# Windowed attention inside a feed-forward stream: nine score blocks in one group over two PSUM banks, values likewise, and the scheduler's constants set anew

## The chip, the core and the metric

The kernel runs on one core of one Trainium2 chip. The metric is the device time of one execution in microseconds (us). PE is TensorE's matmul stream, PEld its weight loads, DVE is VectorE, ACT ScalarE, POOL GpSimd, SP the engine whose queue issues most transfers. PSUM has eight banks of 512 fp32 columns.

## What is computed

Attention over 4 batches of 8 heads (576 positions, 64 columns a head), then two feed-forward layers (512 to 2048 to 512) over the 2304 tokens.

```python
scores = scale * q @ k.T
mask   = 0 <= rel < 32                          # heads 0..3
mask   = 0 <= rel < 128 and rel % 4 == 0        # heads 4..7
attn   = softmax(where(mask, scores, -1e9))
x      = (attn @ v) as tokens x 512
h = x @ w_in1;  x = (h - tanh(h)) @ w_out1
h = x @ w_in2;  y = (h * sigmoid(h)) @ w_out2
```

## The kernel before

**Layers.** Tokens go in blocks of 512 (the last of a layer has 256): blocks 0 to 4 are layer 1, five more are layer 2. For each of 16 slices `f` of the hidden width, a block does 12 matmuls of 512 columns into a bank `h` (four `c` of three passes each, since every operand is held as a high and a low part), a gate on ACT and DVE, and 12 matmuls from `gg` into the four banks `y`. All of these are issued in `passes` (L583).

**Attention.** Two heads make a `Pair`; four pairs make a batch. The 576 positions of a pair are cut into `NB` = 9 blocks of 64 queries by 96 keys. `products` (L444) makes score blocks on PE, one 64x64 matmul per head and block; `masks` (L465) scales and adds the mask on DVE, `maxima` (L468) takes the row maxima, `exps` (L481) the exponentials on ACT, `norm` (L486, L487, L491) divides, `p_transpose` (L504) turns the probabilities on DVE, `values` (L522) multiplies by v on PE, and `x_hi` (copy helper, L135) and `x_lo` (L563) write the result into `X`. Batch 0 goes in units of `UB` = 3 blocks and adds its masks on PE (L437). The later batches work in groups of three score blocks in the single bank of the pool `ps_s`, and values in groups of six and three blocks in the single bank of `ps_o`.

**Order.** Four things set it. Batch 0, block 0, all of batch 1 and the preparation of layer 1's weights (L169, L174, L179, L183, L135, L192: four engines take each chunk apart into high and low parts) are operations `op(...)` with an assumed cost per engine and a rank; `play` emits them in the order of a greedy schedule. While a bank is lent for it, `play` fills assumed idle time of PE with dummy matmuls (`idle`, L97). Batches 2 and 3 are laid into the stream of blocks 1 to 3 by `plan`: `STARTS` gives each pair's first tick (a tick is half a slice, 12 layer matmuls), `STEPS` the ticks of its steps after that. Before everything, `WARM` dummy matmuls (L799) run on PE. Weight chunks wait in staging buffers, one fixed and the others named by `MORE_OUT` and `MORE_IN`.

```python
at(s0 + score + u, lambda u=u: p.scores(u))
at(s0 + exp + u, lambda u=u: p.exps(u))
...
at(s0 + out, lambda: p.outputs(0, 2 * UB))
at(s0 + out + 1, lambda: p.outputs(2 * UB, NB))
```

Of the kernel before, what the change touches and what calls it, by code (L numbers as in the profile page):

```python
# [19 lines left out]
P = 128  # L20
# [3 lines left out]
UB = 3  # L24
# [8 lines left out]
def tile_kernel(  # L33
# [223 lines left out]
    tpool = attn.enter_context(tc.tile_pool(name="tiny", bufs=4))  # L257
# [7 lines left out]
    one = {}  # L265
    for dt in (F32, BF16):
        t = cpool.tile([P, P], dt, name=f"one{len(one)}")
        nc.gpsimd.memset(t, 0.0)
        keep(t, [[-1, P]], 0, 1, fill=1.0, op=ALU.not_equal)
        one[dt] = t  # L270


    mask = cpool.tile([P, NB + 2, KB], BF16, name="mask")
# [3 lines left out]
    keep(half, [[0, NB + 2], [-1, KB]], HALO, 1)  # L277
    keep(half, [[0, NB + 2], [1, KB]], -1, -1)
    for n in range(NB):

        for start in range(0, S, CLS):
            at = start - (QB * n - HALO)
# [5 lines left out]
    mask_dil = [mask[:, UB * u:UB * (u + 1)] for u in range(NU)]  # L288
    mask_plain = [mask[:, 0::5]] + [mask[:, NB - 1:]] * (NU - 1)

    late = cpool.tile([P, NC, SHIFT], F32, name="late")
# [5 lines left out]
    class Pair:  # L297
# [132 lines left out]
        def part(self, t, u):  # L430
            return t[:, UB * u:UB * (u + 1)]

        def products(self, bank, u, masked):
            s = bank[:, :UB * KB].rearrange("p (n k) -> p n k", n=UB)
            mk = (mask_dil if self.dil else mask_plain)[u]
            if masked:
                nc.tensor.matmul(s, one[BF16], mk, start=True, stop=False)  # L437
            for m in range(UB):
                n = UB * u + m
                k0 = QB * n - HALO  # L440

                for at, k1, size in ((0, k0, KB),) if n else ((0, 0, HALO), (HALO, 0, KB - HALO))[masked:]:
                    for j in range(2):
# [4 lines left out]
                            start=not masked, stop=not masked or m == UB - 1,  # L448
                        )
            if u == 0:  # L450
                self.p = ppool.tile([P, NB, KB], F32, tag="p", name="prob")
                self.total = tpool.tile([P, NB], F32, tag="sum", name="sum", bufs=2)
            self.nb[u] = tpool.tile([P, UB], F32, tag="nb", name="nb")
# [3 lines left out]
        def masked_scores(self, u, bank):  # L457
            self.ps[u], _ = self.products(bank, u, True)

        def plain_scores(self, u):  # L460
            self.ps[u] = self.products(ps_s.tile([P, 512], F32, tag="s", name="s"), u, False)

        def masks(self, u):
            s, mk = self.ps.pop(u)
            nc.vector.scalar_tensor_tensor(out=self.part(self.p, u), in0=s, scalar=SCALE, in1=mk, op0=ALU.mult, op1=ALU.add)  # L465

        def maxima(self, u):
            nc.vector.tensor_reduce(out=self.nb[u], in_=self.ps[u] if u in self.ps else self.part(self.p, u), axis=AX.X, op=ALU.max, negate=True)  # L468


        def scores(self, u):
            self.plain_scores(u)
            self.masks(u)
            self.maxima(u)

        def exps(self, u):
            s, nb = self.ps.pop(u, None), self.nb.pop(u)
            for m in range(UB):
                n = UB * u + m
# [262 lines left out]
    def plan(p, s0):  # L742
# [23 lines left out]
    with tc.manual_schedule():  # L766
# [60 lines left out]
        for i, (p, u) in enumerate(units):  # L827
# [27 lines left out]
            a = op({"T": 0.5}, lambda e, p=p, u=u, i=i: p.values(UB * u, UB * (u + 1), *((ps_s, "s") if i % 2 else (ps_o, "o"))),  # L855
# [46 lines left out]
        left_s = left_o = tuple(x_done[NPAIR - 1][-2:])  # L902
        left_pT = tuple(ring_v.take() + ring_v.take() + ring_v.take())
        left_qT = left_kT = left_v = ()
        left_v = (first[2].last,)
        x_next = []
        todo_v = None
        for p in pairs[NPAIR:2 * NPAIR + 1]:
            r = NEXT0 + NEXT * p.c + (NEXT * NPAIR if p.b > 1 else 0)
            q_in = op({"S": 2.2}, lambda e, p=p: p.load_q(), left_qT, r - 12, 2.0)  # L910
            k_in = op({"S": 2.2}, lambda e, p=p: p.load_k(), left_kT, r - 12, 2.0)
            hold = op({"P": 0.2}, lambda e, p=p: p.v_tile(), left_v, r - 5)
            v_in = [op({"S": 0.55}, fn, [hold], r - 5 + 0.01 * n, 0.4) for n, fn in enumerate(p.v_loads())]
            if p.b > 1:
                break
            a = op({"V": 1.09}, lambda e, p=p: p.transpose(0), [q_in, *left_qT], r)
            b = op({"V": 1.09}, lambda e, p=p: p.transpose(1), [k_in, *left_kT], r)
            free_p = ring_p.take()
            exps, scores = [], []
            for u in range(NU):  # L920
                c = op({"T": 0.65}, lambda e, p=p, u=u: p.plain_scores(u), [a, b, *left_s, *free_p], r + 2 + 2 * u)
                scores.append(c)
                d = op({"V": 0.46}, lambda e, p=p, u=u: p.masks(u), [c], r + 2 + 2 * u)
                left_s = (d,)
                d = op({"V": 0.4}, lambda e, p=p, u=u: p.maxima(u), [d], r + 2 + 2 * u)
                exps.append(op({"A": 1.35}, lambda e, p=p, u=u: p.exps(u), [d], r + 3 + 2 * u))
            left_qT = left_kT = tuple(scores)
            left_qT, left_kT = (a, *scores), (b, *scores)
            c = op({"V": 0.4}, lambda e, p=p: p.sums(0, NB), exps, r + 9)
            c = op({"V": 1.0, "P": 1.64}, lambda e, p=p: p.normed(e, 0, NB), [c], r + 9, port=True)  # L930
            ts = [op({"V": 0.4}, lambda e, p=p, j=j, n=n: p.p_quarter(j, n), [c, *left_pT], r + 11 + 0.5 * n)
                  for j in range(2) for n in range(4)]
            ring_p.leave(*ts)
            vals = []
            for n0, n1 in ((0, 2 * UB), (2 * UB, NB)):
                m = (n1 - n0) / NB
                a = op({"T": 1.5 * m}, lambda e, p=p, n0=n0, n1=n1: p.values(n0, n1), [*ts, *v_in, *left_o], r + 14)
                vals.append(a)
                b = op({"A": 0.2 + m}, lambda e, p=p, n0=n0: p.x_hi(e, n0), [a], r + 15)
                c = op({"V": 0.2 + m}, lambda e, p=p, n0=n0: p.x_lo(n0), [b], r + 15)  # L940
                left_o = (c,)
                x_next.append(c)
            left_pT = tuple(vals)
            left_v = tuple(vals)
# [22 lines left out]
        for f in range(NF):  # L967
# [17 lines left out]
            for f2 in ([f - 1] if f else []) + ([f] if f == NF - 1 else []):  # L985
                pass
        for f in range(NF - 2):
            prev = second[f - 1][-1:] if f else [x for p in (first[-1],) for x in x_done[NPAIR - 1]]
            for c in range(NC):
# [107 lines left out]
```

## Time and profile before

| what | us |
|---|---|
| median of 3 runs (lowest, highest) | 903.54 (903.01, 904.36) |
| the profiled execution's own time | 905.87 |
| its span, first to last instruction | 904.1 |
| PE busy | 887.0 (98%) |
| DVE, ACT, POOL busy | 423.2, 386.5, 130.2 |

The profiled execution lies 2.3 us above the median, and its span is 1.8 us shorter than its own time. The stretches of the span: 0 to 48.6 is batch 0; 48.6 to 162 is block 0 with batch 1 and the weight preparation; 162 to 362 holds blocks 1 to 3 with batches 2 and 3; from there the layers run alone.

### The profile page before, as it was taken

The numbers are of one execution on the slowest core, as the hardware profiler recorded it, in microseconds if no ns is written. First come the engines' busy times: TensorE is split into PE (matmuls) and PEld (weight loads), VectorE is DVE, ScalarE is ACT, GpSimd is POOL, SyncE is SP. The second block draws the span as 40 slices with busy tenths as digits, with TensorE's granted clock in tenths as the row PEclk, the third lists the DMA queues.
The fourth block names the chain that finished last, engine by engine and source line by source line (L and its number), as shares of the span: only waits on it lengthen the run. The fifth ranks groups of instructions, "written<-read, shape, count | busy, mean of one in ns | idle before, by whom it ended". The sixth has DMA issues, their size and how long they took to land.

```text
span 904.1 us, 13656 instructions
## 1 busy us (share of the span) xinstructions
PE 887.0 (98%) x5260; PEld 726.9 (80%) x5260; DVE 423.2 (47%) x782; ACT 386.5 (43%) x927; POOL 130.2 (14%) x168
## 2 busy tenths in 40 slices
PE   8899999999999999999998999999999999999998
PEld 5677777777777778888898888888888888888897
DVE  3569986556666654323365656522222222222232
ACT  5699974433343333332355666432223222322322
POOL 7455652000000000000011222100000000000000
PEclk9799999999999999999999999999999999999999
DMA  9967243421234200400164564140004000300100
GB/s 230 281 180 186 66 122 92 120 47 31 49 67 130 38 9 20 162 1 24 47 219 133 168 213 153 47 140 1 0 1 140 1 0 1 94 1 1 30 18 24
DMA packets 121313, 74.29 MB, mean 82 GB/s; under 512 B 84864, under 2 KB 106400, under 8 KB 121248
## 3 DMA queue, kind: packets, MB, share of 16 engines
q1 hardware_dynamic: 120416, 72.57, 28.7%
q0 software_dynamic: 832, 0.85, 0.4%
q8 instruction: 41, 0.67, 0.3%
q14 instruction: 24, 0.20, 0.1%
HBM read 59.24 MB, written 14.16 MB: 81 GB/s over the span
## 4 chain that ended last, share of the span: by engine, by line
PE 74%; DVE 4%; ACT 2%; DMA 1%; issue 1%; ACTq 0%; DVEq 0%; SPq 0%
PE y L583 36%; PE h L583 35%; PE s L444 2%; PE o L522 1%; DVE pT L504 1%; DVE w L192 1%; DMA st<-in_moe_w_in_dram 1%; DVE g L610 1%; ACT w L135 1%; ACT gg L1057 1%; ACT st L169 0%; DVE gg L1059 0%; DVE st L179 0%; ACT g L609 0%; DVE x L641 0%
## 5 line engine op out<-in xcount | busy, mean ns | idle before, releaser
L583 PE MATMUL h<-x,w 128*128 128x512 f32 (+1 forms) x1920 | 428.3, 370 | 2.5 <-DVE g L610 2.2
L583 PEld LDWEIGHTS h<-x,w 128*128 128x128 f32 x1920 | 335.6, 188 | 65.7 <-DVE g L610 3.1
L583 PE MATMUL y<-gg,w 128*128 128x512 f32 (+1 forms) x960 | 219.4, 372 | 1.3 <-DVE gg L1059 0.7
L583 PE MATMUL y<-w,gg 128*128 128x512 f32 x864 | 209.8, 390 | 0.0
L583 PEld LDWEIGHTS y<-gg,w 128*128 128x128 f32 x960 | 166.3, 188 | 34.4 <-DVE x L641 1.3
L583 PEld LDWEIGHTS y<-w,gg 128*128 128x128 f32 x864 | 160.8, 188 | 33.7 <-ACT gg L1057 0.6
L665 DVE SCALAR_TENSOR_TENSOR g<-g,h 128x512 f32<-128x512 f32 (+1 forms) x80 | 50.6, 633 | 195.8 <-ACT g L664 195.7
L1057 ACT ACTIVATE gg<-g 128x512 fp32r<-128x512 f32 (+1 forms) x144 | 84.2, 585 | 123.1 <-DVE g L610 63.1
L1059 DVE TENSOR_TENSOR gg<-g,gg 128x512 fp32r<-128x512 f32 (+1 forms) x144 | 91.2, 633 | 93.8 <-ACT gg L1057 89.5
L664 ACT ACTIVATE g<-h 128x512 f32<-128x512 f32 (+1 forms) x80 | 44.3, 554 | 196.9 <-PE h L583 196.9
L183 POOL TENSOR_TENSOR st<-st 128x512 int32<-128x512 int32 x64 | 69.5, 1091 | 235.7 <-ACT st L174 196.3
L609 ACT ACTIVATE g<-h 128x512 f32<-128x512 f32 (+1 forms) x64 | 34.7, 543 | 131.5 <-PE h L583 125.7
L610 DVE TENSOR_TENSOR g<-h,g 128x512 f32<-128x512 f32 (+1 forms) x64 | 39.7, 620 | 90.0 <-ACT g L609 89.9
L192 DVE TENSOR_TENSOR w<-st,w 128x512 fp32r<-128x512 f32 x53 | 50.8, 962 | 25.7 <-ACT w L135 25.7
L504 DVE STREAM_TRANSPOSE pT<-prob 32x288 f32<-32x288 f32 x96 | 44.9, 468 | 5.3 <-POOL prob L491 3.9
L169 ACT ACTIVATE st<-st 128x512 f32<-128x512 f32 x64 | 43.1, 673 | 7.6 <-DMA st<-in_moe_w_in_dram 5.0
L135 ACT ACTIVATE w<-st 128x512 fp32r<-128x512 f32 x64 | 42.3, 662 | 2.8 <-POOL st L183 2.8
L174 ACT ACTIVATE st<-st 128x512 int32<-128x512 uint32 x64 | 43.3, 676 | 0.0
L481 ACT ACTIVATE prob<-prob,nb 128x96 f32<-128x96 f32 x108 | 38.9, 366 | 3.5 <-DVE nb L468 3.5
L179 DVE TENSOR_SCALAR st<-st 128x512 uint32<-128x512 uint32 x64 | 27.7, 445 | 7.9 <-ACT st L169 6.5
L491 POOL TENSOR_TENSOR prob<-prob,sum 128x864 f32<-128x864 f32 (+1 forms) x15 | 17.8, 1185 | 87.3 <-DVE sum L487 82.7
L522 PEld LDWEIGHTS o<-pT,v 96*64 96x64 f32 x576 | 21.1, 141 | 11.1 <-issue 6.6
(66 smaller groups left out, 435.1 us busy)
## 6 DMA issues: line engine op xcount, KB each, us to landing
st<-in_moe_w_in_dram SPq DMA_DIRECT2D x64, 256.0 KB
st<-in_moe_w_out_dram SPq DMA_DIRECT2D x32, 512.0 KB
y_hi<-x SPq DMA_DIRECT2D x4, 1024.0 KB
y_lo<-x SPq DMA_DIRECT2D x4, 1024.0 KB
x<-y_hi SPq DMA_DIRECT2D x4, 1024.0 KB
x<-y_lo SPq DMA_DIRECT2D x4, 1024.0 KB
qin<-in_q_dram SPq DMA_DIRECT2D x48, 72.0 KB
kin<-in_k_dram SPq DMA_DIRECT2D x48, 72.0 KB
```

Source lines behind the costliest of these rows:

```text
L135: engine.activation(out=out, in_=in_, func=AF.Copy, scale=1.0 if scale is None else scale)
L169: engine.activation(out=high, in_=high, func=AF.Prelu, scale=2.0 ** -112, alpha=2.0 ** 32)
L174: engine.activation(out=low.bitcast(I32), in_=low, func=AF.Copy, scale=2.0 ** -29)
L183: engine.tensor_tensor(out=high, in0=high, in1=self.low.bitcast(I32), op=ALU.add)
L192: engine.tensor_tensor(out=self.flat[:, 1], in0=self.high.bitcast(F32), in1=self.flat[:, 0].bitcast(F32), op=ALU.subtract)
L504: nc.vector.transpose(out=pT[32 * kk:32 * kk + 32, :, j, 32 * i:32 * i + 32], in_=self.p[p0:p0 + 32, :, 32 * kk:32 * kk + 32],)
L583: nc.tensor.matmul(o, stat[a], mov[b], start=first and n == 0, stop=last and n == 2)
L610: nc.vector.tensor_tensor(out=g, in0=h, in1=g, op=ALU.subtract)
L664: nc.scalar.activation(out=g, in_=h, func=AF.Tanh, scale=0.5)
L665: nc.vector.scalar_tensor_tensor(out=g, in0=g, scalar=1.0, in1=h, op0=ALU.add, op1=ALU.mult)
L1057: nc.scalar.activation(out=gg[:, 0], in_=g, func=AF.Copy)
L1059: nc.vector.tensor_tensor(out=gg[:, 1], in0=g, in1=gg[:, 0].bitcast(F32), op=ALU.subtract)
```

## The change

From batch 1 on, a pair's nine score blocks are issued as one run on PE: blocks 0 to 4 into the bank of `ps_s`, blocks 5 to 8 into the bank of `ps_o` (`GROUPS`). DVE and ACT then do masks, maxima and exponentials per group of five and four, where they did them per three. The nine value blocks are issued as one run over the same two banks. The mask array gets 14 rows instead of 11, so that a slice of it serves either group. In the planner a pair has a `front` (scores to norm) and a `back` (transposes, values), and the front of pair n+1 is listed ahead of the back of pair n. The constants: 12 warm-up matmuls for 18, three staging buffers in `MORE_OUT` for four, 0.2 us more assumed idle time from 12 us on (`LESS_IDLE`), other `STARTS`, and `STEPS` with norm and turn one tick earlier. The fp32 identity shares the buffer `late`.

```diff
-                idle(t - free[e] + (MORE_IDLE if t < 12.0 else 0.0))
+                idle(t - free[e] + (MORE_IDLE if t < 12.0 else LESS_IDLE))
...
+    GROUPS = ((0, (NB + 1) // 2), ((NB + 1) // 2, NB))
+    NM = NB + GROUPS[0][1]
+    mask = cpool.tile([P, NM, KB], BF16, name="mask")
...
+        def bank(self, n0):
+            return (ps_o if n0 else ps_s).tile([P, 512], F32, tag="o" if n0 else "s", name="o" if n0 else "s")
+        def plain_scores(self):
+            for n0, n1 in GROUPS:
+                self.ps[n0] = self.products(self.bank(n0), n0, n1, False)
...
-        def scores(self, u):
-            self.plain_scores(u)
-            self.masks(u)
-            self.maxima(u)
+        def scores(self):
+            self.plain_scores()
+            for g in GROUPS:
+                self.masks(*g)
+                self.maxima(*g)
...
-        def outputs(self, n0, n1):
-            self.values(n0, n1)
-            self.x_hi(nc.scalar, n0)
-            self.x_lo(n0)
+        def all_values(self):
+            for n0, n1 in GROUPS:
+                self.values(n0, n1, self.bank(n0))
+        def outputs(self):
+            self.all_values()
+            for n0, _ in GROUPS:
+                self.x_hi(nc.scalar, n0)
+                self.x_lo(n0)
...
-    STARTS = ((33, 40, 46, 52), (59, 66, 74, 81))
-    STEPS = (1, 3, 4, 7, 8, 11)
+    STARTS = ((35, 41, 46, 52), (61, 65, 71, 80))
+    STEPS = (1, 3, 4, 6, 7, 11)
...
-    MORE_OUT = (27, 29, 30, 31)
+    MORE_OUT = (29, 30, 31)
-    WARM = 18
+    WARM = 12
+    LESS_IDLE = 0.2
...
-            for u in range(NU):
-                c = op({"T": 0.65}, lambda e, p=p, u=u: p.plain_scores(u), [a, b, *left_s, *free_p], r + 2 + 2 * u)
+            c = op({"T": 2.1}, lambda e, p=p: p.plain_scores(), [a, b, *left["bank"], *ring_p.take()], r + 2)
...
+            a = op({"T": 1.45}, lambda e, p=p: p.all_values(), [*ts, *v_in, *left["bank"]], r + 14)
...
+        for n, p in enumerate(new[:-1]):
+            front(new[n + 1])
+            back(p)
```

PE's order in the steady stretch (batch 2; `s` and `o` are the two attention banks, `h` and `y` the layer's), before:

```order
L583 MATMUL h<-x,w 128x512 x12
L522 MATMUL o<-pT,v 64x64 x12
L444 MATMUL s<-kT,qT 64x96 x6
L583 MATMUL y_2033<-gg,w 128x512 x3
L583 MATMUL y_2034<-gg,w 128x512 x3
L583 MATMUL y_2035<-gg,w 128x512 x3
L583 MATMUL y_2036<-gg,w 128x512 x3
L522 MATMUL o<-pT,v 64x64 x6
L444 MATMUL s<-kT,qT 64x96 x6
L583 MATMUL h<-x,w 128x512 x12
```

and of the change, at the same batch:

```order
L593 MATMUL h<-x,w 128x512 x12
L443 MATMUL s<-kT,qT 64x32 x2
L443 MATMUL s<-kT,qT 64x64 x2
L443 MATMUL s<-kT,qT 64x96 x8
L443 MATMUL o<-kT,qT 64x96 x8
L593 MATMUL y_1999<-gg,w 128x512 x3
L593 MATMUL y_2000<-gg,w 128x512 x3
L593 MATMUL y_2001<-gg,w 128x512 x3
L593 MATMUL y_2002<-gg,w 128x512 x3
L593 MATMUL h<-x,w 128x512 x12
```

The three places of scores and the two of values have become one place each. (A row counts matmuls as written; the profile shows two records for each of these fp32 ones.) Over the whole order, attention of batches 1 to 3 stands between layer matmuls at 46 places before and at 24 places in the change.

PE's order where block 0 starts with batch 1's first pair, before:

```order
L583 MATMUL h<-x,w 128x512 x18
L444 MATMUL s<-kT,qT 64x32 x2
L444 MATMUL s<-kT,qT 64x64 x2
L444 MATMUL s<-kT,qT 64x96 x4
L583 MATMUL h<-x,w 128x512 x3
L583 MATMUL y_911<-gg,w 128x512 x3
L583 MATMUL y_912<-gg,w 128x512 x3
L444 MATMUL s<-kT,qT 64x96 x6
```

and of the change:

```order
L593 MATMUL h<-x,w 128x512 x9
L97 LDWEIGHTS one
L97 MATMUL y_715<-mask,one 128x224
L97 LDWEIGHTS one
L97 MATMUL y_715<-mask,one 128x224
L593 MATMUL h<-x,w 128x512 x3
L443 MATMUL s<-kT,qT 64x32 x2
L443 MATMUL s<-kT,qT 64x64 x2
L443 MATMUL s<-kT,qT 64x96 x8
L443 MATMUL o<-kT,qT 64x96 x8
L593 MATMUL h<-x,w 128x512 x9
```

Two dummy matmuls now stand here, and nine more behind the last row; before, none stood behind the first layer matmul. In the opening, 34 stand where 26 stood.

## Rows read from the trace of the kernel before

**Rows 1.** Timeline of PE, steady stretch (start us, us, engine, line, what)
```profile
187.34 2.88 PE L583 MATMUL y<-gg,w 128*128 128x512 f32 x12
190.18 0.78 PE L444 MATMUL s<-kT,qT 64*64 64x32 f32 x16
190.89 3.01 PE L583 MATMUL h<-x,w 128*128 128x512 f32 x12
193.84 1.10 PE L522 MATMUL o<-pT,v 96*64 96x64 f32 x24
194.87 0.71 PE L444 MATMUL s<-kT,qT 64*64 64x96 f32 x12
195.51 3.02 PE L583 MATMUL y<-gg,w 128*128 128x512 f32 x12
198.46 0.57 PE L522 MATMUL o<-pT,v 96*64 96x64 f32 x12
198.96 0.71 PE L444 MATMUL s<-kT,qT 64*64 64x96 f32 x12
199.60 3.06 PE L583 MATMUL h<-x,w 128*128 128x512 f32 x12
202.49 2.88 PE L583 MATMUL y<-gg,w 128*128 128x512 f32 x12
```

**Rows 2.** Chain of waits, from 362 us: start us, us, what
```profile
365.38 2.72 PE h L583 x12
```

**Rows 3.** Timeline of PE, a value group of 24 alone
```profile
218.72 0.92 PE L522 MATMUL o<-pT,v 96*64 96x64 f32 x24
219.57 0.71 PE L444 MATMUL s<-kT,qT 64*64 64x96 f32 x12
```

**Rows 4.** Layer matmuls (L583) alone by stretch, PE
```profile
48.60:162.00 113.40, 98.77 (x408) 1.00 0.50 129
162.00:362.00 200.00, 171.38 (x719) 1.00 0.26 56
```

**Rows 5.** PE's waits from 48 to 362 us: total, times, longest
```profile
PE s L444 <- DVE prob L465: 1.3, 2, 0.7
PE o L522 <- DVE x L563: 1.2, 1, 1.2
```

**Rows 6.** By stretch: us, then PE, PEld, DVE, ACT, POOL busy
```profile
75.00:100.00 25.00, 25.00 (x167) 19.30 (x166) 23.83 (x49) 23.82 (x66) 12.00 (x12) 1.00 0.63 166
125.00:150.00 25.00, 24.15 (x151) 18.55 (x149) 19.51 (x39) 17.57 (x45) 12.73 (x14) 1.00 0.42 105
162.00:362.00 200.00, 197.21 (x1327) 156.16 (x1327) 119.88 (x231) 72.56 (x241) 13.03 (x21) 1.00 0.26 56
```

**Rows 7.** Timeline, all engines, 55 to 57 us
```profile
55.33 0.68 DVE L192 TENSOR_TENSOR w<-st,w 128x512 fp32r<-128x512 f32 x1
...
56.12 1.08 PE L583 MATMUL y<-gg,w 128*128 128x512 f32 x4
```

**Rows 8.** Timeline of PE, a filler run
```profile
44.77 1.21 PE L97 MATMUL y<-mask,one 128*128 128x224 bf16 x11 [1.59 <-ACT prob L481]
```

**Rows 9.** The opening: timelines of PE and of ACT
```profile
1.47 6.20 PE L799 MATMUL y<-warm 128*128 128x512 bf16 x18 [1.47 <-DVE warm L795]
7.60 1.21 PE L408 MATMUL h<-one,qin 96*64 96x96 f32 x24
...
9.57 1.07 ACT L285 COPY mask<-mask 64x1056 bf16<-64x1056 bf16 x1
```

**Rows 10.** By stretch, the slow clock; then the timeline of PE
```profile
29.60:39.90 10.30, 10.30 (x99) 7.63 (x98) 5.15 (x18) 5.38 (x26) 4.01 (x6) 0.51 1.06 336
...
35.94 0.45 PE L437 MATMUL y<-mask,one 128*128 128x288 bf16 x1
...
39.05 0.45 PE L437 MATMUL y<-mask,one 128*128 128x288 bf16 x1
...
41.28 0.29 PE L437 MATMUL y<-mask,one 128*128 128x288 bf16 x1
```

More of the change, by code (lines that the diff above doesn't have):

```diff
@@ L256, in tile_kernel @@
     ppool = attn.enter_context(tc.tile_pool(name="p", bufs=2))
-    tpool = attn.enter_context(tc.tile_pool(name="tiny", bufs=4))
+    tpool = attn.enter_context(tc.tile_pool(name="tiny", bufs=2))
     ps_s = attn.enter_context(tc.tile_pool(name="ps_s", bufs=1, space=PSUM))
@@ L263, in keep @@
                                 fill=fill, base=base, channel_multiplier=mult)
-    one = {}
-    for dt in (F32, BF16):
-        t = cpool.tile([P, P], dt, name=f"one{len(one)}")
+    late = cpool.tile([P, NC, SHIFT], F32, name="late")
+    one = {F32: late[:, 0], BF16: cpool.tile([P, P], BF16, name="one")}
+    for t in one.values():
         nc.gpsimd.memset(t, 0.0)
         keep(t, [[-1, P]], 0, 1, fill=1.0, op=ALU.not_equal)
-        one[dt] = t
-    mask = cpool.tile([P, NB + 2, KB], BF16, name="mask")
+    GROUPS = ((0, (NB + 1) // 2), ((NB + 1) // 2, NB))
+    NM = NB + GROUPS[0][1]
+    mask = cpool.tile([P, NM, KB], BF16, name="mask")
     nc.gpsimd.memset(mask[0:QB], 0.0)
     half = mask[0:QB]
[L277 to L282, printed above, removed]
+    keep(half, [[0, NM], [-1, KB]], HALO, 1)
+    keep(half, [[0, NM], [1, KB]], -1, -1)
+    for n in range(NB + 1):
+        for start in range(0, S, CLS) if n < NB else (0,):
+            at = start - (QB * (n % NB) - HALO)
             if 0 < at < KB:
@@ L287, in tile_kernel @@
     lent = []
-    mask_dil = [mask[:, UB * u:UB * (u + 1)] for u in range(NU)]
-    mask_plain = [mask[:, 0::5]] + [mask[:, NB - 1:]] * (NU - 1)
-    late = cpool.tile([P, NC, SHIFT], F32, name="late")
     kT1 = cpool.tile([P, S], F32, name="kT")
@@ L428, in transpose, with products @@
             nc.vector.transpose(out=dst, in_=src)
[L430 to L435, printed above, removed]
+        def products(self, bank, n0, n1, masked):
+            s = bank[:, :(n1 - n0) * KB].rearrange("p (n k) -> p n k", k=KB)
+            a = n0 if self.dil else NB + (n0 > 0)
+            mk = mask[:, a:a + n1 - n0]
             if masked:
                 nc.tensor.matmul(s, one[BF16], mk, start=True, stop=False)
-            for m in range(UB):
-                n = UB * u + m
+            for n in range(n0, n1):
+                m = n - n0
                 k0 = QB * n - HALO
@@ L447, in products @@
                             self.kT[64 * j:64 * j + 64, k1:k1 + size],
-                            start=not masked, stop=not masked or m == UB - 1,
+                            start=not masked, stop=not masked or n == n1 - 1,
                         )
-            if u == 0:
+            if n0 == 0:
                 self.p = ppool.tile([P, NB, KB], F32, tag="p", name="prob")
-                self.total = tpool.tile([P, NB], F32, tag="sum", name="sum", bufs=2)
-            self.nb[u] = tpool.tile([P, UB], F32, tag="nb", name="nb")
+                self.tiny = tpool.tile([P, 2 * NB], F32, tag="sum", name="sum")
+                self.total = self.tiny[:, :NB]
@@ L454, in products @@
+            self.nb[n0] = self.tiny[:, NB + n0:NB + n1]
             return s, mk
[L457 to L465, printed above, removed]
@@ L467, in maxima, with masked_scores @@
-        def maxima(self, u):
-            nc.vector.tensor_reduce(out=self.nb[u], in_=self.ps[u] if u in self.ps else self.part(self.p, u), axis=AX.X, op=ALU.max, negate=True)
-        def scores(self, u):
-            self.plain_scores(u)
-            self.masks(u)
-            self.maxima(u)
[L476 to L479, printed above, removed]
+        def masked_scores(self, n0, n1, bank):
+            self.ps[n0], _ = self.products(bank, n0, n1, True)
@@ new lines, in bank, with masks, maxima @@
+        def bank(self, n0):
[3 more added lines that the diff above has]
+                self.ps[n0] = self.products(self.bank(n0), n0, n1, False)
+        def masks(self, n0, n1):
+            s, mk = self.ps.pop(n0)
+            nc.vector.scalar_tensor_tensor(out=self.p[:, n0:n1], in0=s, scalar=SCALE, in1=mk, op0=ALU.mult, op1=ALU.add)
+        def maxima(self, n0, n1):
+            nc.vector.tensor_reduce(out=self.nb[n0], in_=self.ps[n0] if n0 in self.ps else self.p[:, n0:n1], axis=AX.X, op=ALU.max, negate=True)
@@ L480, in exps @@
+        def scores(self):
[3 more added lines that the diff above has]
+                self.maxima(*g)
+        def exps(self, n0, n1):
+            s, nb = self.ps.pop(n0, None), self.nb.pop(n0)
+            for m in range(n1 - n0):
+                n = n0 + m
                 pr = self.p[:, n, :]
@@ L515, in p_copy, with values @@
         def p_copy(self, engine, u):
-            copy(engine, self.part(pT, u).rearrange("p n j q -> p n (j q)"), self.pt.pop(u))
-        def values(self, n0, n1, pool=None, tag="o"):
-            o = (pool or ps_o).tile([P, 512], F32, tag=tag, name="o")[:, :(n1 - n0) * QB].rearrange("p (n q) -> p n q", q=QB)
+            copy(engine, pT[:, UB * u:UB * (u + 1)].rearrange("p n j q -> p n (j q)"), self.pt.pop(u))
+        def values(self, n0, n1, bank):
+            o = bank[:, :(n1 - n0) * QB].rearrange("p (n q) -> p n q", q=QB)
             for n in range(n0, n1):
@@ L749, in plan @@
             at(s0 + two, lambda: pairs[n].load())
-        for u in range(NU):
-            at(s0 + score + u, lambda u=u: p.scores(u))
-            at(s0 + exp + u, lambda u=u: p.exps(u))
+        at(s0 + score, p.scores)
+        for k, g in enumerate(GROUPS):
+            at(s0 + exp + k, lambda g=g: p.exps(*g))
         at(s0 + norm, p.norm)
@@ L755, in plan @@
         at(s0 + turn + 1, lambda: p.p_transpose(1))
-        at(s0 + out, lambda: p.outputs(0, 2 * UB))
-        at(s0 + out + 1, lambda: p.outputs(2 * UB, NB))
+        at(s0 + out, p.outputs)
         if n < len(pairs):
-            at(s0 + out + 1, lambda: pairs[n].load_v())
+            at(s0 + out, lambda: pairs[n].load_v())
     for b in range(2, B):
@@ L854, in tile_kernel @@
             ring_t.leave(m)
-            a = op({"T": 0.5}, lambda e, p=p, u=u, i=i: p.values(UB * u, UB * (u + 1), *((ps_s, "s") if i % 2 else (ps_o, "o"))),
+            a = op({"T": 0.5}, lambda e, p=p, u=u, i=i: p.values(UB * u, UB * (u + 1), p.bank(1 - i % 2)),
                    [m, *got[p, "v"], *ring_o.take()], r)
@@ L899, in tile_kernel @@
                 in_room[NF - len(MORE_IN) + place - 1 - len(MORE_OUT)] = (c,)
[L902 to L908, printed above, removed]
+        left = {"bank": tuple(x_done[NPAIR - 1][-2:]), "pT": tuple(ring_v.take() + ring_v.take() + ring_v.take()),
+                "q": (), "k": (), "v": (first[2].last,)}
@@ L909, in tile_kernel, with front @@
+        normed = {}
+        def front(p):
             r = NEXT0 + NEXT * p.c + (NEXT * NPAIR if p.b > 1 else 0)
[L910 to L913, printed above, removed]
+            q_in = op({"S": 2.2}, lambda e, p=p: p.load_q(), left["q"], r - 12, 2.0)
+            k_in = op({"S": 2.2}, lambda e, p=p: p.load_k(), left["k"], r - 12, 2.0)
@@ L914, in tile_kernel @@
             if p.b > 1:
[L915 to L920, printed above, removed]
-                c = op({"T": 0.65}, lambda e, p=p, u=u: p.plain_scores(u), [a, b, *left_s, *free_p], r + 2 + 2 * u)
[L922 to L926, printed above, removed]
@@ L927, in tile_kernel @@
[L927 to L931 removed]
+                return
+            a = op({"V": 1.09}, lambda e, p=p: p.transpose(0), [q_in, *left["q"]], r)
@@ new lines, in front @@
+            b = op({"V": 1.09}, lambda e, p=p: p.transpose(1), [k_in, *left["k"]], r)
+            c = op({"T": 2.1}, lambda e, p=p: p.plain_scores(), [a, b, *left["bank"], *ring_p.take()], r + 2)
+            left["q"], left["k"] = (a, c), (b, c)
+            left["bank"], exps = (), []
+            for n0, n1 in GROUPS:
+                m = (n1 - n0) / NB
+                d = op({"V": 0.1 + m}, lambda e, p=p, g=(n0, n1): p.masks(*g), [c], r + 2 + 4 * n0 / NB)
+                left["bank"] += (d,)
+                d = op({"V": 0.1 + m}, lambda e, p=p, g=(n0, n1): p.maxima(*g), [d], r + 2 + 4 * n0 / NB)
+                exps.append(op({"A": 4.1 * m}, lambda e, p=p, g=(n0, n1): p.exps(*g), [d], r + 4 + 4 * n0 / NB))
@@ new lines, in front, with v_of, back @@
+            c = op({"V": 0.4}, lambda e, p=p: p.sums(0, NB), exps, r + 9)
+            normed[p] = op({"V": 1.0, "P": 1.64}, lambda e, p=p: p.normed(e, 0, NB), [c], r + 9, port=True)
+        def v_of(p):
+            r = NEXT0 + NEXT * p.c + (NEXT * NPAIR if p.b > 1 else 0)
+            hold = op({"P": 0.2}, lambda e, p=p: p.v_tile(), left["v"], r - 5)
+            return [op({"S": 0.55}, fn, [hold], r - 5 + 0.01 * n, 0.4) for n, fn in enumerate(p.v_loads())]
+        def back(p):
+            r = NEXT0 + NEXT * p.c
+            v_in = v_of(p)
+            ts = [op({"V": 0.4}, lambda e, p=p, j=j, n=n: p.p_quarter(j, n), [normed[p], *left["pT"]], r + 11 + 0.5 * n)
@@ L932, in tile_kernel @@
                   for j in range(2) for n in range(4)]
             ring_p.leave(*ts)
-            vals = []
-            for n0, n1 in ((0, 2 * UB), (2 * UB, NB)):
+            a = op({"T": 1.45}, lambda e, p=p: p.all_values(), [*ts, *v_in, *left["bank"]], r + 14)
+            left["pT"] = left["v"] = (a,)
+            left["bank"] = ()
+            for n0, n1 in GROUPS:
                 m = (n1 - n0) / NB
-                a = op({"T": 1.5 * m}, lambda e, p=p, n0=n0, n1=n1: p.values(n0, n1), [*ts, *v_in, *left_o], r + 14)
-                vals.append(a)
@@ L939, in tile_kernel @@
                 b = op({"A": 0.2 + m}, lambda e, p=p, n0=n0: p.x_hi(e, n0), [a], r + 15)
[L940 to L944, printed above, removed]
+                left["bank"] += (op({"V": 0.2 + m}, lambda e, p=p, n0=n0: p.x_lo(n0), [b], r + 15),)
+        new = pairs[NPAIR:2 * NPAIR + 1]
+        front(new[0])
+        for n, p in enumerate(new[:-1]):
+            front(new[n + 1])
+            back(p)
@@ L947, in tile_kernel @@
+        v_of(new[-1])
         waiting = []
@@ L984, in tile_kernel @@
             second.append([])
[L985 to L989, printed above, removed]
+            prev = second[f - 1][-1:] if f else x_done[NPAIR - 1]
+            for c in range(NC if f < NF - 2 else 0):
                 second[f].append(op({"T": 0.69}, lambda e, f=f, c=c: blk.second_part(f, c, state["gg"][:, f % 2, :, :blk.n]),
```

6 lines of the change are left out of this document (3 added, 3 removed).

## The prediction

> **What bounds the kernel now.** I read the span cut into stretches first, then PE's waits, then the timeline of PE where attention cuts into the layer stream. The stretches say that PE is the bound from 48.6 us on: it is busy 25.00 of 25 us at 75 to 100 and 197.21 of 200 at 162 to 362 [rows 6]. A busy PE is not yet a PE at its pace, so the pace has to come from elsewhere: undisturbed, twelve layer matmuls take 2.72 us [rows 2], 0.2267 us each. The stretch 162 to 362 holds 719 layer matmuls [rows 4], which would take 163.0 us, so 37.0 us go to attention and its side effects. The stretch 48.6 to 162 holds 408, 92.5 us, so 20.9 us go the same way. These 57.9 us are what the change can touch in the stream. The rest is the opening of 48.6 us, which it also touches, and the layers after 362, which it doesn't.
>
> **What one place of attention costs.** In the timeline of PE [rows 1] four layer groups and one pair's places run from 187.34 to 202.49, 15.15 us, where four groups alone take 10.88: 4.27 us for that pair. The pieces: the score runs hold PE for 190.89 - 190.18 = 0.71 (16 records) and 195.51 - 194.87 = 0.64 and 199.60 - 198.96 = 0.64 (12 records each). The value run of 12 holds it for 198.96 - 198.46 = 0.50, that of 24 for 219.57 - 218.72 = 0.85 [rows 3]. So 12 more value records cost 0.35, and 0.50 - 0.35 = 0.15 of a run is start and end. A layer group next to such a place lasts 2.95 (190.89 to 193.84, 195.51 to 198.46) where 2.72 is its pace: 0.23 per place, outside the attention matmuls.
>
> **The change in the stream, term by term.** No score or value matmul is removed. One run of scores has 16 + 12 + 12 records: 0.71 + 2 x (0.64 - 0.15) = 1.69, taking for a score run the 0.15 that value runs show. One run of values has 36: 0.85 + 0.35 = 1.20. With two places at 0.23 a pair costs 3.35 us. If the score runs had no such 0.15 to save, 3.65.
>
> *162 to 362 (eight pairs).* 8 x 3.35 = 26.8 against 37.0: 10.2 us less, 7.8 with the 3.65. Part of the 37.0 is waiting: PE waited 1.3 us for masks to leave the single score bank [rows 5]. Two banks remove that wait, but a larger group can bring another, so I let 1.8 us of waits stay: **-8.4**. DVE's four larger operations per pair in place of six lie beside layer matmuls, since DVE is busy 119.88 of 200 us; if that cover is gone, the next gate is late, and then PE.
>
> *48.6 to 162 (four pairs).* 4 x 3.35 = 13.4, plus the last value run of batch 0 with its place, 0.73, plus eleven dummy matmuls at 1.21 / 11 = 0.11 [rows 8] and 0.23 for each of their two places, 1.7: 15.8 against 20.9, 5.1 less. Here PE has a partner. ACT is busy 23.82 of 25 us at 75 to 100, and weights come just in time: the low half of one is written from 55.33 to 56.01, and the `y` group starts at 56.12 [rows 7]. In that part ACT has about 5% to give. At 125 to 150 it is busy 17.57 of 25, so there it can follow. Bounds: 0 (the weights bind all of it) and -5.1. Also in the 20.9 is the wait of 1.2 us of a value run for its single bank [rows 5], which the second bank removes. I take two thirds, **-3.4**, since only the first half is full. One staging buffer less is in this bound too: it delays a transfer, and the wait would be a weight's.
>
> *The opening.* PE goes from the warm-up straight into the q transposes (1.47 + 6.20 = 7.67; they start at 7.60), so six fewer of 18 let them start earlier, by 6.20 / 3 = 2.1 us at most. Against it: the mask copy on ACT stands ahead of the k copies, 1.07 us, and grows by 14/11, 0.3 us [rows 9]; eight more dummies are 0.9 us if none falls into idle time. Later the opening waits for transfers and for ACT chains, which eat an early start. I take **-0.5**, between -2.1 and +1.2, the clock aside (a rival).
>
> **Sum:** -8.4 - 3.4 - 0.5 = -12.3. The span of 904.1 becomes 891.8, the profiled execution's own 905.87 becomes 893.6, and the median of 903.54 becomes **891.2**. Identity in `late`, `tiny` with two buffers and the new mask slices add no instruction on the path.
>
> **Rivals.**
>
> *Two banks held by one group make each group wait for the one before (slower).* Scores now take both attention banks, and so do values: scores of the next pair wait until `x_lo` has read the values, values wait until `masks` has read the scores. The place is the bank change at each of the 24 runs. The price row is PE's wait of 1.2 us, where the second value group waited for `x_lo` of the first one [rows 5]. At 1.2 us each it is 28.8 us: 903.5 - 12.3 + 28.8 = 920. It decides from 12.3 / 24 = 0.51 us per run on. Against it: such waits sum to 2.5 us over 314 us now, though the steps share one bank each and often follow at the next tick, and in the new constants the runs are two or more ticks apart except at two places. The Trainium skill ("Perfetto Trace Analysis", Optimizing Tensor Performance) says that independent matmul groups should rotate through different PSUM banks, so that the evacuation of one overlaps the next group's matmuls. By that rule this rival would come true; no run here shows yet a group that takes both banks, and the kernel before, which reuses one bank at once, pays 2.5 us for it.
>
> *Weights bind block 0.* If ACT can't follow, the -3.4 is gone: 903.5 - 8.9 = 894.6, and with the 3.65 of a pair 897.
>
> *The clock in the opening.* From 29.6 to 39.9 PE had the clock of 1.2 GHz (granted 0.51 on average, busy 10.30 of 10.30). A unit of batch 0 took 39.05 - 35.94 = 3.11 us there and 41.28 - 39.05 = 2.23 after [rows 10]. 10.3 / 3.11 = 3.3 units, times 0.88, is 2.9 us. More dummies may keep the clock, 888.3, or a shorter warm-up may lose it a second time, 894.1.
>
> **How the numbers follow.** The forecast (886 to 896) 0.62; weights bind (893 to 899) 0.18; the clock kept (884 to 889) 0.09; bank waits (over 905) 0.07; gains used up by several small waits (within 0.2%, 1.8 us, about what a measurement can tell here) 0.04. The range 884.5 to 899 leaves out the last two and some of the third's tail. Faster 0.89, same 0.04, slower 0.07.
>
> **What would show it.** Right: in the profile after, the stretch of batches 2 and 3 loses about 8 us, a score run holds PE for about 1.7 us and a value run for 1.2, a pair's two places cost about 3.4, and no PE wait for `x_lo` or `masks` stands in the list above 1 us in all. The first layer matmul stands near 48. Block 0 is 3 to 4 us shorter with DVE or ACT ops of weights ahead of PE's only gaps. Wrong: `s` and `o` runs with idle time ahead of them released by DVE; a place that costs far from 0.23; block 0 unchanged with PE waiting for `w`; a first layer matmul past 50 or before 46.

## The result and the profile after

The changed kernel takes 891.95 us (median of 4 runs, 889.73 to 893.78), beside 903.88 (4 runs, 903.01 to 904.36) for the kernel before: a ratio of 0.9868, interval 0.9842 to 0.9894. That is 11.9 us less; the forecast was 12.3 less, 891.2. The profiled execution lasted 889.73, its span 888.0.

The page of the changed kernel, its busy line (share, instructions):

```profile
PE 874.0 (98%) x5273; PEld 724.6 (82%) x5273; DVE 422.5 (48%) x761; ACT 387.1 (44%) x925; POOL 127.3 (14%) x166
```

DVE and ACT work as much as before (422.5 and 387.1 us, 423.2 and 386.5 before); PE is busy 13.0 us less, though no matmul of attention was removed. (3.6 of the 13.0 lie in the opening, where the low clock lasted 10.2 us in this profile of the kernel before and 3.4 in that of the changed one.) Where the time came from shows when both traces are cut at the same layer matmul. Block b begins at its first matmul into `h`. The table is worked out from the traces' records; "again" are second profiles of the two kernels, run later.

| us | before | before again | changed | changed again |
|---|---|---|---|---|
| opening, to the start of block 0 | 48.66 | 44.06 | 44.93 | 45.02 |
| block 0 | 102.20 | 102.22 | 99.14 | 98.97 |
| blocks 1 and 2 (batches 2 and 3 lie here) | 214.36 | 214.35 | 206.19 | 206.23 |
| block 3 to the middle of block 4 | 111.47 | 111.47 | 111.47 | 111.48 |
| from there to layer 2 | 26.26 | 26.59 | 25.11 | 26.34 |
| layer 2 to the end | 401.14 | 401.37 | 401.12 | 401.12 |

The rows of block 0 and of blocks 1 and 2 repeat to 0.2 us in these pairs. They hold the change: -3.1 to -3.2 in block 0 and -8.1 to -8.2 in blocks 1 and 2. Four variants below (e1, e2, e4, e5) leave block 0 as it is in the changed kernel, and it takes 98.66 to 98.71 us there, so over six profiles block 0 is 3.1 to 3.6 shorter, and the two rows together 11.2 to 11.7. The opening differs by 4.6 us between two executions of one program; the row ahead of layer 2 moves by 1.2 between executions of one program too. Neither can carry a conclusion from one pair of profiles.

The timeline of PE in the changed kernel, in the stretch of [rows 1] (start us, us, engine, line, what):

```profile
185.37 1.11 PE L443 MATMUL s<-kT,qT 64*64 64x32 f32 x24
186.28 0.86 PE L443 MATMUL o<-kT,qT 64*64 64x96 f32 x16
187.07 3.02 PE L593 MATMUL y<-gg,w 128*128 128x512 f32 x12
189.93 2.88 PE L593 MATMUL h<-x,w 128*128 128x512 f32 x12
192.74 0.80 PE L527 MATMUL s<-pT,v 96*64 96x64 f32 x20
193.37 0.64 PE L527 MATMUL o<-pT,v 96*64 96x64 f32 x16
193.94 3.02 PE L593 MATMUL y<-gg,w 128*128 128x512 f32 x12
...
202.32 1.11 PE L443 MATMUL s<-kT,qT 64*64 64x32 f32 x24
```

From one score run to the next, 185.37 to 202.32, are 16.95 us with five layer groups. At 2.72 each [rows 2] these are 13.60, so the pair costs 3.35, where it was 4.27. (A place, below, is a run of attention matmuls between two layer matmuls.) The score run holds PE for 187.07 - 185.37 = 1.70, the value run for 193.94 - 192.74 = 1.20; the layer group behind each lasts 2.86 and 2.85 instead of 2.72, and the one ahead of the value run 2.81 (189.93 to 192.74), so 0.22 to 0.23 lie beside a run. All eight score runs of blocks 1 and 2 hold PE for 1.70 and all eight value runs for 1.20, by the starts in the trace.

The same stretch on DVE shows why no bank is waited for (rows of the masks and of `x_lo`):

```profile
189.20 0.65 DVE L469 SCALAR_TENSOR_TENSOR prob<-s,mask 128x480 f32<-128x480 f32 x1
...
190.45 0.55 DVE L469 SCALAR_TENSOR_TENSOR prob<-o,mask 128x384 f32<-128x384 f32 x1
...
195.55 0.74 DVE L568 TENSOR_TENSOR x<-s,x 128x80 fp32r<-128x80 f32 x2
196.14 0.50 DVE L568 TENSOR_TENSOR x<-o,x 128x192 fp32r<-128x192 f32 x1
```

The masks have read both banks by 190.45 + 0.55 = 191.00, and the value run starts at 192.74: 1.7 us to spare. `x_lo` is done at 196.64, and the next scores come at 202.32: 5.7 to spare. PE's waits in the changed kernel from 44 to 350 us (total, times, longest), and the stretches of block 0 and of blocks 1 and 2 (us, then PE, PEld, DVE, ACT, POOL busy, PE's granted clock, DMA share, GB/s), first of the changed kernel, then of the kernel before:

```profile
PE s L443 <- DVE kT L428: 1.0, 1, 1.0
PE y L593 <- DVE gg L1073: 0.7, 1, 0.7
PE y L593 <- DVE w L192: 0.3, 1, 0.3
PE y L593 <- DVE gg L977: 0.2, 1, 0.2
```

```profile
44.93:144.07 99.14, 98.54 (x692) 78.63 (x688) 86.53 (x164) 86.05 (x212) 50.75 (x51) 1.00 0.58 152
144.07:350.26 206.19, 204.39 (x1390) 166.88 (x1388) 124.69 (x226) 79.41 (x251) 13.48 (x22) 1.00 0.25 56
...
48.66:150.86 102.20, 100.77 (x681) 78.08 (x677) 86.13 (x171) 87.65 (x213) 55.06 (x52) 1.00 0.52 134
150.86:365.22 214.36, 211.57 (x1393) 167.73 (x1389) 125.69 (x241) 77.70 (x251) 13.60 (x24) 1.00 0.25 56
```

The waits for `masks` and `x_lo` of [rows 5], 2.5 us, are gone. The longest left is one of 1.0 for the transposed keys of batch 3's third pair, which starts three ticks earlier than it did. PE is shown as busy 99% of both stretches, as before, and most of the gain lies inside that busy time: 2.2 us in block 0 and 7.2 in blocks 1 and 2. Idle time gives the other 0.8 and 1.0.

### The profile page after: what moved, and what is told of

It is laid out like the page before. It is cut to its first block, busy times and chain, and to the rows that moved or that the text cites. A ratio compares the mean times of both kernels' runs of the same rounds, so it can differ in the third digit from the quotient of the medians.

```text
span 888.0 us, 13675 instructions
## 1 busy us (share of the span) xinstructions
PE 874.0 (98%) x5273; PEld 724.6 (82%) x5273; DVE 422.5 (48%) x761; ACT 387.1 (44%) x925; POOL 127.3 (14%) x166
## 4 chain that ended last, share of the span: by engine, by line
PE 85%; DVE 8%; ACT 4%; issue 1%; DMA 1%; POOL 0%; DVEq 0%; ACTq 0%; POOLq 0%
PE h L593 39%; PE y L593 39%; DVE w L192 2%; DVE pT L509 2%; PE s L527 1%; PE s L443 1%; DMA st<-in_moe_w_in_dram 1%; DVE g L620 1%; PE y L443 1%; PE o L527 1%; DVE st L179 1%; PE o L443 1%; ACT w L135 1%; PE y L97 1%; ACT st L169 1%
## 5 line engine op out<-in xcount | busy, mean ns | idle before, releaser
L183 POOL TENSOR_TENSOR st<-st 128x512 int32<-128x512 int32 x64 | 67.5, 1060 | 237.2 <-ACT st L174 211.3
L192 DVE TENSOR_TENSOR w<-st,w 128x512 fp32r<-128x512 f32 x56 | 52.7, 948 | 28.7 <-ACT w L135 28.6
L486 ACT ACTIVATE prob<-prob,sum 128x96 f32<-128x96 f32 x108 | 38.9, 365 | 10.2 <-DVE sum L472 10.2
L496 POOL TENSOR_TENSOR prob<-prob,sum 128x864 f32<-128x864 f32 (+1 forms) x17 | 21.3, 1253 | 86.4 <-DVE sum L492 85.3
L486 ACT ACTIVATION_READ_ACCUMULATOR prob<-prob,sum 128x1 f32 x108 | 20.7, 191 | 0.0
```

The lines of the kernel that those rows point to most:

```text
L183: engine.tensor_tensor(out=high, in0=high, in1=self.low.bitcast(I32), op=ALU.add)
L192: engine.tensor_tensor(out=self.flat[:, 1], in0=self.high.bitcast(F32), in1=self.flat[:, 0].bitcast(F32), op=ALU.subtract)
L486: nc.scalar.activation(out=pr, in_=pr if s is None else s[:, m, :], func=AF.Exp, bias=nb[:, m:m + 1], accum_out=self.total[:, n:n + 1])
```

## The experiments

In e1 to e6 one thing is changed against the changed kernel; e7 and e8 are the two kernels again. Kernels e1 to e4 shared one set of runs of the kernel before (902.68, 14 runs), e5 to e8 another (903.25, 7 runs). Beside the time, each is read by the length of block 0 (98.66 to 99.14 in the six profiles named above) and of blocks 1 and 2 (206.19 and 206.23 in the changed kernel).

**e1: the groups at two ticks each, in batches 2 and 3.** The two banks and all starts stay; the loads of the next pair's v go one tick later, with the second value group. Where batch 2's last pair writes its second value group, block 2 has begun to read its tokens, so those columns are old there.

```diff
-        at(s0 + score, p.scores)
         for k, g in enumerate(GROUPS):
+            at(s0 + score + k, lambda g=g: p.scores(g))
...
-        at(s0 + out, p.outputs)
+        for k, g in enumerate(GROUPS):
+            at(s0 + out + k, lambda g=g: p.outputs(*g))
```

> The changed kernel with one thing undone in batches 2 and 3: a pair's score groups of five and four blocks stand at two following ticks, and so do its two value groups; batch 1, banks, group sizes and constants stay as changed. Theory (a place of attention in the layer stream costs a fixed time): 16 more places at 0.23 us outside the runs and 0.15 inside, 6.1 us more in the stretch of batches 2 and 3, nothing elsewhere. Rival (the gain came from fewer waits for banks and from the placement): the places are free, under 1 us.

Measured: 899.72 (897.84 to 901.46), ratio to the kernel before 0.9962 (0.9946 to 0.9977). Blocks 1 and 2 take 213.20, 7.0 more. PE's timeline:

```profile
185.49 1.11 PE L443 MATMUL s<-kT,qT 64*64 64x32 f32 x24
186.53 3.04 PE L593 MATMUL y<-gg,w 128*128 128x512 f32 x12
189.49 0.88 PE L443 MATMUL o<-kT,qT 64*64 64x96 f32 x16
190.30 3.06 PE L593 MATMUL h<-x,w 128*128 128x512 f32 x12
193.29 0.80 PE L527 MATMUL s<-pT,v 96*64 96x64 f32 x20
194.02 3.02 PE L593 MATMUL y<-gg,w 128*128 128x512 f32 x12
196.97 0.69 PE L527 MATMUL o<-pT,v 96*64 96x64 f32 x16
...
203.25 1.11 PE L443 MATMUL s<-kT,qT 64*64 64x32 f32 x24
```

From score run to score run 17.76 us with five layer groups: 4.16 for the pair, 0.81 more than 3.35, so 0.40 for each of two more places. The whole of blocks 1 and 2 (columns as above), and from PE's waits the one there that is attention's:

```profile
143.78:356.98 213.20, 210.17 (x1390) 166.62 (x1389) 125.55 (x226) 80.53 (x251) 13.24 (x22) 1.00 0.24 54
...
PE o L527 <- DVE pT L509: 2.3, 1, 2.3
```

PE's busy time grows by 210.17 - 204.39 = 5.8 us, its idle time by 1.2 (3.03 beside 1.80), since one value run now waits 2.3 us for the turned probabilities. So the places cost 5.8 of the 7.0. The trace has 30 places instead of 16, not 32, since a value group and the next scores share a tick twice: by the forecast's 0.23 outside and 0.15 inside, 14 x 0.23 + 16 x 0.15 = 5.6. The same matmuls, divided among more places, give most of the gain of this stretch back.

**e2: the starts and steps of the kernel before.**

```diff
-    STARTS = ((35, 41, 46, 52), (61, 65, 71, 80))
-    STEPS = (1, 3, 4, 6, 7, 11)
+    STARTS = ((33, 40, 46, 52), (59, 66, 74, 81))
+    STEPS = (1, 3, 4, 7, 8, 11)
```

> The changed kernel with STARTS and STEPS of before: the groups over two banks stay, but a pair's values now follow the next pair's scores at the next tick or share one with them, four times or more. If two banks held by one group make each group wait for the one before, every such neighbour costs 0.5 to 1.2 us, 3 to 8 us in the stretch of batches 2 and 3. By the theory that the places alone count, places that share a tick even save 0.23: within 1.5 us of the changed kernel.

Measured: 894.89 (893.0 to 895.72), ratio 0.9906 (0.9888 to 0.9924); blocks 1 and 2 take 209.60, 3.4 more. PE's longest waits from 144 to 408 us, and in its timeline one place of the second wait, then that of the first:

```profile
PE s L443 <- DVE x L568: 2.3, 1, 2.3
PE o L527 <- DVE prob L469: 0.7, 3, 0.2
```

```profile
250.40 0.80 PE L527 MATMUL s<-pT,v 96*64 96x64 f32 x20
251.45 0.69 PE L527 MATMUL o<-pT,v 96*64 96x64 f32 x16 [0.25 <-DVE prob L469]
252.07 3.02 PE L593 MATMUL h<-x,w 128*128 128x512 f32 x12
...
295.11 0.64 PE L527 MATMUL o<-pT,v 96*64 96x64 f32 x16
298.04 1.11 PE L443 MATMUL s<-kT,qT 64*64 64x32 f32 x24 [2.29 <-DVE x L568]
```

At one tick scores follow values at once. They wait 2.29 us until `x_lo` has left the bank: the bank rival. At four places values follow scores by one tick. There the value run holds PE for 1.27, 1.67 (252.07 - 250.40), 1.72 and 1.67 us instead of 1.20, of which only three waits of 0.2 for the masks are shown as idle. Together these five value runs hold PE 3.9 us longer, the wait of 2.29 included, and the stretch is 3.4 longer. The two banks want other ticks, and the new ones are worth 3.4 us.

**e5: the same groups at the same ticks, all through one bank.**

```diff
         def scores(self):
-            self.plain_scores()
             for g in GROUPS:
+                self.ps[g[0]] = self.products(self.bank(0), *g, False)
                 self.masks(*g)
                 self.maxima(*g)
...
-            self.all_values()
-            for n0, _ in GROUPS:
+            for n0, n1 in GROUPS:
+                self.values(n0, n1, self.bank(0))
                 self.x_hi(nc.scalar, n0)
```

> The changed kernel, but batches 2 and 3 put both groups of a run, one after the other, into the single bank of ps_s (the other attention bank stays empty); the place count stays at 16 there. By the theory that the places alone set the cost, nothing changes, under 1 us. If the second bank is what makes a single place possible, PE stands in each run until the first group has been read: about 0.8 us for masks in each of 8 score runs and 2 us for copies and differences in each of 8 value runs, 20 us or more in the stretch of batches 2 and 3.

Measured: 949.64 (948.35 to 961.19), ratio 1.0563 (1.0491 to 1.0635). Blocks 1 and 2 take 263.0, 56.8 more. PE's waits, a place of the timeline, and PE's busy time in a stretch, with the granted clock behind its count:

```profile
PE s L443 <- DVE prob L469: 20.9, 8, 4.6
PE s L527 <- DVE x L568: 17.1, 8, 2.9
```

```profile
204.99 1.12 PE L527 MATMUL s<-pT,v 96*64 96x64 f32 x16 [2.85 <-DVE x L568]
206.04 5.45 PE L593 MATMUL y<-gg,w 128*128 128x512 f32 x12
211.33 2.92 PE L593 MATMUL h<-x,w 128*128 128x512 f32 x12
```

```profile
204.50:211.33 6.83, 6.34 (x29) 0.50 0.41 85
```

Each of the sixteen runs waits once inside, 38.0 us in all, or 2.4 per run: 2.6 for masks, where 0.8 was expected, and 2.1 for `x_lo`. The clock brings the rest: behind the wait of 2.85 us a layer group takes 206.04 to 211.33, 5.29 us and about twice its 2.72, at 1.2 GHz. The trace's clock records have eight low stretches in blocks 1 and 2, 3.4 or 6.8 us each, 37.5 in all, and PE was busy in 35.5 of them. At half the clock, half of that, 17.8, is lost, of the 56.8 - 38.0 = 18.8 to explain. So the second bank is what makes one run possible. The Trainium skill ("Perfetto Trace Analysis", Optimizing Tensor Performance) advises to rotate independent matmul groups through different PSUM banks, so that one group is read while the next is written. The trace of e5 agrees: with both groups in one bank, PE waits these 38.0 us. The prediction feared that a run over two banks would break the same rule. In the changed kernel no run waits for a bank, though the next run comes one tick later at two places (scores behind values) and two or more ticks later at the others.

**e3: no added assumed idle time.**

```diff
-    LESS_IDLE = 0.2
+    LESS_IDLE = 0.0
```

> The changed kernel with LESS_IDLE at 0, so without most of the dummy matmuls behind the warm-up. In block 0 their 11 go: 1.7 us less there if PE is the bound at those two places, nothing if PE would have waited in them. In the opening: if the dummies keep the clock at 2.4 GHz, the opening gets longer by 2 to 4 us and the granted clock of the run falls; if they don't matter to it, the opening stays within 1 us.

Measured: 890.1 (888.67 to 892.55), ratio 0.9855 (0.9832 to 0.9877), not to be told from the changed kernel. The trace shows that the edit removes fewer dummies than expected: eight of the eleven in block 0 still run, in one place instead of two, and 26 of the 34 in the opening. Block 0 takes 98.48, 0.2 to 0.7 less than in the six profiles. That bounds three dummies and one place, priced at 0.33 + 0.23; the 1.7 for all eleven is not tested. The first layer matmul stands at 46.05, within the spread of the unchanged opening (44.93 to 46.59, see e4), so the opening shows no price of eight dummies either. PE's timeline at the end of the opening:

```profile
40.49 1.93 PE L97 MATMUL y<-mask,one 128*128 128x224 bf16 x11 [1.59 <-ACT prob L486]
```

Eleven dummies in 1.93 us where [rows 8] has 1.21: the low clock came here, as it did in the first profile of the changed kernel with its additional dummies (below).

**e4: the longer warm-up.**

```diff
-    WARM = 12
+    WARM = 18
```

> The changed kernel with 18 warm-up matmuls again. If the opening's 3.7 us came from the earlier start, the first layer matmul comes 1.2 to 1.5 us later and the rest of the 3.7 belongs to the clock. If it came from the clock alone, the start is eaten by later waits and the first layer matmul moves by less than 0.5 us at the same clock.

Measured: 890.81 (889.78 to 893.62), ratio 0.9867 (0.9846 to 0.9888). The q transposes start at 7.64, where e8, whose low clock comes at nearly the same time (11.9 us beside 12.8), has 5.93. Of these 1.7 us only 0.6 are left at the first layer matmul (45.60 beside 45.02), and five profiles whose opening is unchanged (the changed kernel, e1, e2, e5, e8) have 44.93, 45.10, 46.59, 46.15 and 45.02 there. A warm-up worth 0.6 us can't be told apart from that spread. Besides, e8 has a stall of 0.88 us there that e4 lacks (see e7 and e8), so by an estimate from the two profiles the six warm-up matmuls cost 0.6 to 1.5.

**e6: weights without the low-half step on ACT.** The step is left out for layer 1's 32 chunks; layer 2's 32 keep it, other than the expectation says. All layer weights become zero.

```diff
-            engine.tensor_tensor(out=high, in0=high, in1=self.low.bitcast(I32), op=ALU.add)
+            engine.tensor_tensor(out=high, in0=high, in1=high, op=ALU.subtract)
...
-            c = op({"A": 0.58}, lambda e, ch=ch: ch.lows(e), [a], due, port=True)
+            c = op({"A": 0.58}, lambda e: None, [a], due, port=True)
```

> The changed kernel with the ACT step of the low weight halves (64 instructions of layers 1 and 2) left out and the POOL step joining the high half with itself, so the weights are zero; every other instruction stands where it stood. ACT has some 20 us less in block 0. If weights and ACT bound block 0 (the reason given for taking 3.4 of 5.1 us), block 0 gets 1.5 to 2.5 us shorter, 99.1 to about 97. If PE bounds it alone, it stays within 0.5 us.

Measured: 890.51 (888.89 to 892.39), ratio 0.9869 (0.9847 to 0.9891). The beginning of block 0, first of the changed kernel, then of e6, and the whole of block 0 in e6 (columns as above):

```profile
45.00:70.00 25.00, 25.00 (x188) 20.00 (x189) 21.20 (x37) 24.41 (x59) 14.91 (x14) 1.00 0.80 203
```

```profile
45.00:70.00 25.00, 25.00 (x189) 20.21 (x189) 21.92 (x37) 19.56 (x47) 15.96 (x13) 1.00 0.82 210
...
44.17:142.06 97.89, 97.80 (x692) 78.86 (x688) 87.41 (x164) 70.28 (x181) 51.08 (x51) 1.00 0.58 152
```

ACT's load falls from 24.41 to 19.56 of the first 25 us, and from 86.05 to 70.28 in the whole block. Block 0 becomes 97.89 us, shorter than in the six profiles by 0.8 to 1.3, between the two expectations. PE's waits for `w` and `gg`, 0.5 us in the list above, are no longer there, and PE is idle for 0.1 us in all. So ACT and the weights hold about 1 us of block 0; no other partner shows as idle time of PE. The zero weights don't change PE's own pace: blocks 1 and 2, on the same zero weights, take 206.15 us.

**e7 and e8: the kernels before and after once more.** No edit.

> The kernel before, profiled once more. If the opening's 3.7 us between the two profiles belongs to the change, the first layer matmul stands near 48.7 again whatever the clock did. If it belongs to how long the clock was low in one execution, the opening is shorter with a shorter low stretch: 46 or less at a span of about 900, and everything from block 0 on keeps its lengths.

> The changed kernel once more, beside the kernel before in the same call. Median of its runs 890 to 893. Opening 45 to 48 by the length of the low clock, block 0 near 99.1, blocks 1 and 2 near 206.2.

Measured: e7 901.83 in its one run, e8 890.38 (889.74 to 890.93), ratio 0.9866 (0.9849 to 0.9884). The windows of 11 to 16 us have the same granted clock in both, and a later one of the first profile of the changed kernel has it low:

```profile
11.00:16.00 5.00, 4.97 (x62) 3.91 (x62) 1.28 (x3) 3.18 (x14) 3.90 (x7) 0.66 0.99 215
```

```profile
11.00:16.00 5.00, 5.00 (x64) 4.16 (x66) 2.77 (x8) 2.64 (x13) 3.92 (x8) 0.66 1.02 255
```

```profile
39.50:42.90 3.40, 3.40 (x21) 0.51 0.59 93
```

One program has its low clock for 10.3 us at 30 [rows 10] in one execution and for 3.4 us at 12 in another (0.66 over 5 us); the changed kernel has it at 39.6 and at 12 (in the third row only PE's busy time stands before the clock). At an equal clock the openings compare so, first PE's timeline of e7, then of e8:

```profile
7.24 1.21 PE L408 MATMUL h<-one,qin 96*64 96x96 f32 x24
...
26.64 0.29 PE L437 MATMUL y<-mask,one 128*128 128x288 bf16 x1
...
33.09 0.28 PE L437 MATMUL y<-mask,one 128*128 128x288 bf16 x1
...
44.06 0.98 PE L583 MATMUL h<-x,w 128*128 128x512 f32 x3
```

```profile
5.93 1.21 PE L408 MATMUL h<-late,qin 96*64 96x96 f32 x24
...
25.29 0.29 PE L436 MATMUL y<-mask,one 128*128 128x288 bf16 x1
...
27.81 0.39 PE L527 MATMUL o<-pT,v 96*64 96x64 f32 x7 [0.88 <-issue]
...
32.99 0.28 PE L436 MATMUL y<-mask,one 128*128 128x288 bf16 x1
...
45.02 0.96 PE L593 MATMUL h<-x,w 128*128 128x512 f32 x3
```

The start is 1.3 us earlier with the change, and at the seventh unit of batch 0 all of it is still there (25.29 beside 26.64). Then e8 has a stall of 0.88 us at 27, and at the tenth unit only 0.1 is left (32.99 beside 33.09). Behind that unit stand eight dummies more than before, priced at 0.9, and at the first layer matmul e8 is 1.0 later. The stall is not the change's: the first profile of the kernel before has one of 1.04 us at 28, while e7 and the first profile of the changed kernel have none, nor has e4. In all, seven of the ten profiles have one, of 0.4 to 1.5 us at 26 to 28. Its cause was not found.

## Why the prediction was right, step by step

- **What one place costs** (3.35 us per pair, with 1.69, 1.20 and 0.23): 3.35, 1.70, 1.20 and 0.22 to 0.23 measured. e1, which divides the runs and leaves the rest, gives 7.0 us back, 5.8 of them PE's busy time at 14 more places and 16 more runs. Shown. The 3.65 that stood against it (no start and end to save inside a score run) is excluded.
- **162 to 362, -8.4:** -8.1 to -8.2. The 1.8 us that the sum left for waits are also 1.8 (206.19 - 204.39 idle), which is luck: it was a guess at waits that a larger group might bring, and those that stand there are for `kT` and `gg`, none for a bank.
- **Block 0, -3.4 between 0 and -5.1:** -3.1 to -3.6. The reason, a partner that holds part of it, is about half confirmed: e6 takes 0.8 to 1.3 us out where the full -5.1 would have left 1.5 to 2.0 to find. What holds the rest is not shown. That the weights bind all of it (894.6) is excluded. The price of 1.7 for the dummies is in this bound and stays untested, since e3 removed only three of the eleven.
- **The opening, -0.5:** not settled. The first profiles say -3.7, and the low clock, 10.3 us of it before and 3.4 after, stands in them; the pair at an equal clock says +1.0, of which 0.9 are a stall that is not the change's; five profiles of this opening spread over 1.7. Timed runs in which the mean granted clock was alike, 0.997 to 0.998, leave little for it: median 902.0 for the kernel before (11 runs, 900.52 to 903.27) and 890.1 for the changed one (5 runs, 889.73 to 891.12). Of these 11.9 us the blocks explain 11.2 to 11.7, so a gain of 0.2 to 0.7 is left for the opening and the row ahead of layer 2, less than the spread of the runs. The forecast let later waits eat the early start. In e8 it lasts to 25 us instead, and the stall and the added dummies use it up. One sign of being wrong came true, a first layer matmul before 46 (44.93 and 45.02). It had been set by one profile of the kernel before, whose own second profile has 44.06, so it says nothing of the change.
- **The bank rival** (920): not in this kernel, but a real mechanism. Its single price of 1.2 was wrong, since the price hangs on the distance between runs. Two ticks apart it is nothing, and also where scores follow values by one tick (twice in the changed kernel). Where values follow scores by one tick it is 0.1 to 0.5, and 2.4 where scores follow values at the same tick (e2). Where one bank must serve it is 2.4 per run (e5).
- **The clock rival** (888.3 kept, 894.1 lost): the clock does move the time by some microseconds, from execution to execution of either kernel: the changed kernel took 893.78 at a mean granted clock of 0.993 and 889.73 and 891.12 at 0.997. The dummies don't decide it, as e3 and the two profiles of the changed kernel show; what does was not found.

No run was clearly faster than the changed kernel: e3, e4 and e6 lie within its interval.

## What to carry to other kernels

Where short matmuls of another shape cut into a long stream, count the places, not the matmuls: here each place costs some 0.4 us beyond its matmuls' own pace (0.23 beside the run, 0.15 inside it), and PE is shown as busy throughout. Merging places pays as long as the merged run has banks enough to be written without a reader in between, and the next run comes after its readers: look at when the last reader is done (here 1.7 us ahead) before setting the ticks. Before a difference in an opening is explained, profile both kernels twice. After an edit to a scheduler's constant, count in the trace what it changed: e3 was to remove eleven dummies and removed three.

## What the hardware showed beside

- The low clock's place and length vary between executions of one program: 10.3 us at 30 and 3.4 at 12 for the kernel before, 3.4 at 39.6 and 3.4 at 12 for the changed one. In e6 the opening has none. e3 and e6 have one of 3.4 us at 467 and 466, amid the layers.
- In e5, with sixteen waits of up to 4.6 us, the clock fell to 1.2 GHz eight times in blocks 1 and 2, each time during one of the waits of 2.3 to 4.6 us or within 1.4 us of its end, and cost about half as much as the waits themselves (17.8 and 38.0 us). The changed kernel, with no wait above 1.0 us in blocks 1 and 2, shows no low clock there.
